# Ten steps' probabilities turned by VectorE and HBM instead of TensorE, with a new order of all instructions

## The chip, the cores and the metric

The kernel runs on one core of one Trainium2 chip. The metric is the device time of one execution in microseconds (us), as the median of several runs; less is better. The core's engines have their own queues and wait for each other only through semaphores: TensorE (PE in the profile, its weight loads PEld), VectorE (DVE), ScalarE (ACT), GpSimd (POOL) and SyncE (SP, which only issues transfers).

## What is computed

Four batches of 768 positions go through attention with 8 heads of 64, and the result through a layer of 512 to 1024 to 512.

```python
k_sum = k.reshape(B, H, nb, 32, D).max(axis=3)
v_sum = v.reshape(B, H, nb, 32, D).mean(axis=3)
# local keys: |i - j| < 16; summary keys: 24 blocks of 32
a = softmax(concat([masked q k^T / 8, q k_sum^T / 8 + log(32)]))
x = a @ concat([v, v_sum])              # 3072 rows of 512
h = x @ w_in                            # 512 -> 1024
solu = h * softmax(h)
out = (layernorm(solu) * g_ln) @ w_out  # 1024 -> 512
```

## The kernel before

**Tiles.** The 3072 rows are 24 tiles of 128. The attention has 24 steps: for each batch `b` and each group `g` of four windows of 64 queries there are two steps `pp`, with two head pairs each; step number 2(3b + g) + pp. A step has `scores` (L649): 16 small products of 64 queries against 96 window keys and 24 block maxima, eight reductions on VectorE that add the mask and take the row maximum (L703), eight exponentials with row sums on ScalarE (L715), a reciprocal, and one multiply that normalises all 128 x 960 probabilities `e` (GpSimd or VectorE). `values_turn` (L753) then turns `e` with 16 transposes on TensorE into a PSUM tile `t` (L751), and two copies bring it to `at` in SBUF. `values` (L774) multiplies `at` with the window's values `vt` (x). `combine` (L831) makes the operands of the wide product from x.

**Wide products.** `first` (L950) and `first_two` (L967, for two tiles at once, from tile 6 on) compute h; hu, hl and hf are its three PSUM banks. `solu` (L1025) does softmax, product and layer norm. From tile 4 on the normalised rows go to HBM and come back turned: `send` (L1084) transposes 32 x 32 blocks on VectorE into a staging tile `tb` and writes it to `far`; `fetch` (L1094) reads it back with four transfers into `lt`, and `rows_split` (L1103) splits it into a rounded part `lh` and a rest `ll`. `second_parts` (L1144) is the output product o, 24 wide products a tile. All wide products take three terms for precision, so both weight matrices are split as well: `rounded` (L458) unpacks a weight tile `raw` into `cv` with a shift (L490) and an integer add (L494), and `split_w_in` and `split_w_out` make the two parts `w` of it.

**Order.** Every operation is recorded by `op` with the engines that may do it and a cost. `Plan.ORDER` is a list of all operations' numbers, written out in the kernel, and `Plan.OTHERS` names those that go to another than their first engine. `Plan.order` (L301) walks the list once with the costs; what it computes only decides where `issue` puts filler products (L1350, products of zeros) on TensorE. Each engine then has its instructions in the list's order, and so has SyncE its transfers: an instruction that waits holds up all behind it on its engine. `buf` gives tiles out of rings of fixed size: two `e`, two `at`, one `tb`, two `vrow` (rows whose block means GpSimd adds up, L599, and space for the weights before). SyncE issues the loads and the far transfers; ScalarE issues the output transfers and six small ones.

Of the kernel before, what the change touches and what calls it, by code (L numbers as in the profile page):

```python
# [10 lines left out]
F32 = mybir.dt.float32  # L11
# [9 lines left out]
P = 128  # L21
# [24 lines left out]
FARK, BACK = 1.6, 2.3  # L46
# [7 lines left out]
WPT = 2  # L54

# [7 lines left out]
class Buf:  # L63


    def __init__(self, make, prev=()):
        self.make, self.prev, self.tile = make, prev, None
        self.ops, self.writers, self.readers, self.gone = [], {}, {}, False
# [8 lines left out]
class Op:  # L77
    def __init__(self, can, deps, prio, nbytes, port, land):
        self.can, self.deps, self.engine, self.fn, self.port = can, deps, None, None, port
        self.first = next(iter(can))  # L80
        self.prio, self.nbytes, self.end, self.start = prio, nbytes, None, None
        self.late, self.land = 0.0, land


class Plan:
# [7 lines left out]
    SMALL = 40.0  # L93
    LANDS = (15.0, 0.5), (50.0, 1.4), (1e9, 1.9)
# [5 lines left out]
    ORDER = [35, 2, 4, 5, 8, 6, 7, 12, 3, 1, 21, 13, 23, 0, 137, 22, 14, 25, 24, 138, 9, 27, 40, 15, 26, 42, 29, 41,  # L100
# [105 lines left out]
        "act": (166, 167, 224, 374, 375, 461, 526, 527, 625, 644, 784, 804, 963, 1082, 1083, 1101, 1102, 1241, 1242, 1538,  # L206
            1557, 1669, 1789, 1790),
    }

    def __init__(self):  # L210
# [1184 lines left out]
```

## Time and profile before

| | before |
|---|---|
| median of 3 runs | 354.65 us (354.13 to 354.76) |
| span of the profiled execution | 353.1 us |
| its whole time | not recorded apart; the median lies 1.55 us above this span |
| busy: PE, DVE, ACT, POOL | 344.2, 292.6, 267.9, 195.2 us |
| transfers | 70.29 MB, mean 199 GB/s |

The span runs from the first instruction to the last. Busy time of TensorE counts each product's whole duration, and products overlap, so the chain of waits tells better how long a block of products takes: in the chain, a piece has its start, its length, and the engine and line that the end of the kernel depended on. Rows of a group of instructions give the line, the engine, the tile written and read, the shape, the count, the busy time, and the mean of one in ns. Names keep the program's tile names, with the buffer numbers left out.

### The profile page before, as it was taken

What the parts mean: (1) busy time and instruction counts of PE and PEld (TensorE: products, weight loads), DVE (VectorE), ACT (ScalarE), POOL (GpSimd) and SP (SyncE); (2) the same over time, 40 slices, a digit from 0 to 9 for tenths busy, and PEclk for the clock granted to TensorE, in tenths of its full rate; (3) what the DMA queues carried; (4) which work ended last, traced back from release to release, by engine and by line L of the source; (5) the groups of instructions that cost most, each with busy time, mean ns of one, the idle gap of its engine ahead of it and who ended that gap; (6) DMA issues with size and microseconds to landing.
All of it is one profiled execution on the core that took longest, in us unless ns stands there. A gap on an engine that the chain in (4) does not pass through costs nothing.

```text
span 353.1 us, 9309 instructions
## 1 busy us (share of the span) xinstructions
PE 344.2 (97%) x3253; PEld 271.0 (77%) x3260; DVE 292.6 (83%) x979; ACT 267.9 (76%) x784; POOL 195.2 (55%) x331
## 2 busy tenths in 40 slices
PE   7799999999999999999999999999999999999995
PEld 3347577778777788888888888887887878888885
DVE  3989999999999798889897998987968988966331
ACT  3799999999988988997877785895884886455410
POOL 5133567797895587849598378237336355031500
PEclk9999999999999999999999999999999999999999
DMA  7999995430259577457559742762834543364611
GB/s 270 375 416 403 324 405 188 148 101 22 97 184 317 190 232 230 163 179 234 156 183 292 253 131 106 252 218 81 270 116 156 198 143 121 114 212 154 207 59 61
DMA packets 29970, 70.29 MB, mean 199 GB/s; under 512 B 4012, under 2 KB 14508, under 8 KB 28388
## 3 DMA queue, kind: packets, MB, share of 16 engines
q1 hardware_dynamic: 26060, 62.96, 53.2%
q10 hardware_dynamic: 3864, 6.74, 5.4%
q8 instruction: 26, 0.43, 0.5%
q14 instruction: 20, 0.16, 0.1%
HBM read 50.60 MB, written 16.78 MB: 191 GB/s over the span
## 4 chain that ended last, share of the span: by engine, by line
PE 88%; DVE 5%; DMA 3%; SPq 1%; issue 1%; POOL 0%; DVEq 0%
PE o L1157 35%; PE hu L980 14%; PE h L961 8%; PE hl L980 7%; PE x L808 6%; PE s L682 6%; PE t L751 4%; PE hf L980 3%; DMA st_v<-in_vr 3%; PE x L1350 1%; PE vs_ps L569 1%; DVE e L703 1%; DVE he L1052 1%; DVE ws_own L383 1%; DVE cv L383 1%
## 5 line engine op out<-in xcount | busy, mean ns | idle before, releaser
L1157 PE MATMUL o<-w,lh 128*128 128x512 f32 (+1 forms) x400 | 131.0, 386 | 0.0
L1157 PEld LDWEIGHTS o<-w,lh 128*128 128x128 f32 x400 | 74.1, 188 | 15.7 <-DVE he L1052 0.2
L1157 PE MATMUL o<-w,ll 128*128 128x512 f32 (+1 forms) x200 | 76.3, 381 | 0.0
L715 ACT ACTIVATE e<-e,nm 128x120 f32<-128x120 f32 x192 | 73.3, 388 | 1.9 <-DVE nm L703 1.7
L1157 PEld LDWEIGHTS o<-w,ll 128*128 128x128 f32 x200 | 37.6, 188 | 6.6
L703 DVE CUSTOM_DVE_ANT_0 e<-s,mask 128x120 f32<-128x120 f32 x192 | 40.7, 276 | 1.5 <-PE s L682 1.3
L384 POOL TENSOR_TENSOR e<-e,z 128x960 f32<-128x960 f32 x15 | 28.1, 1873 | 19.5 <-DVE z L728 18.6
L715 ACT ACTIVATION_READ_ACCUMULATOR e<-e,nm 128x1 f32 x192 | 37.0, 193 | 0.0
L961 PE MATMUL h<-w,xh 128*128 128x512 f32 x96 | 33.6, 405 | 0.0
L384 POOL TENSOR_TENSOR ll<-lt,lh 128x512 fp32r<-128x512 f32 x18 | 23.7, 1322 | 15.9 <-ACT lh L376 14.2
L376 ACT CAST lh<-lt 128x512 fp32r<-128x512 f32 x39 | 23.0, 612 | 8.5 <-PE o L1157 4.0
L1044 ACT ACTIVATE he<-hs,hm 128x512 f32<-128x512 f32 x27 | 19.4, 721 | 12.5 <-DVE hm L1033 12.4
L376 ACT COPY at<-t 120x512 f32<-120x512 f32 x40 | 21.8, 590 | 8.2 <-PE t L751 8.0
L1087 DVE STREAM_TRANSPOSE tbl<-he 128x1024 f32<-128x1024 f32 x20 | 24.7, 1233 | 3.2 <-ACT he L1064 1.7
L808 PEld LDWEIGHTS x<-at,vt 120*64 120x64 f32 (+1 forms) x768 | 24.2, 138 | 3.9 <-issue 3.2
L808 PE MATMUL x<-at,vt 120*64 120x64 f32 (+1 forms) x768 | 26.1, 224 | 0.0
L1067 ACT ACTIVATE sq<-he 128x1024 bf16<-128x1024 f32 x24 | 25.3, 1055 | 0.4
L1165 ACT ACTIVATE os<-o,y 128x512 f32<-128x512 f32 x21 | 14.3, 682 | 14.5 <-PE o L1157 8.9
L384 POOL TENSOR_TENSOR xl<-sums,xh 128x256 fp32r<-128x256 f32 (+1 forms) x14 | 12.6, 899 | 21.3 <-DVE xh L377 18.5
L383 DVE TENSOR_TENSOR ll<-lt,lh 128x512 fp32r<-128x512 f32 x22 | 16.8, 779 | 9.0 <-ACT lh L376 8.9
L1071 POOL TENSOR_SCALAR ss<-ss 128x1 f32<-128x1 f32 x24 | 6.2, 259 | 30.3 <-ACT sq L1067 28.9
L611 POOL TENSOR_TENSOR st_v<-st_v 96x512 f32<-96x512 f32 (+3 forms) x28 | 22.4, 803 | 0.5
(184 smaller groups left out, 863.2 us busy)
## 6 DMA issues: line engine op xcount, KB each, us to landing
vt<-in_v SPq DMA_DIRECT2D x12, 1024.0 KB
farl<-tbl SPq DMA_DIRECT2D x20, 512.0 KB
lt<-farl SPq DMA_DIRECT2D x80, 128.0 KB
kraw<-in_k SPq DMA_DIRECT2D x16, 400.0 KB
out<-os ACTq DMA_DIRECT2D x23, 256.0 KB
qt<-in_q SPq DMA_DIRECT2D x11, 512.0 KB
raw<-in_w_in SPq DMA_DIRECT2D x8, 512.0 KB
raw<-in_w_out SPq DMA_DIRECT2D x8, 512.0 KB
```

The lines of the kernel that those rows point to most:

```text
L376: by = {act: lambda: nc.scalar.copy(out=to(), in_=of()), dve: lambda: nc.vector.tensor_copy(out=to(), in_=of()), pool: lambda: nc.gpsimd.t ...
L383: by = {dve: lambda: nc.vector.tensor_tensor(out=to(), in0=a(), in1=b(), op=kind), pool: lambda: nc.gpsimd.tensor_tensor(out=to(), in0=a() ...
L384: pool: lambda: nc.gpsimd.tensor_tensor(out=to(), in0=a(), in1=b(), op=kind)}
L611: op(pool, 0.15 + w * 0.0021, lambda w=w, o=o: nc.gpsimd.tensor_tensor(out=o.ap[:n, :w], in0=x.ap[:n, :w], in1=x.ap[:n, w:2 * w], op=ALU.add),
L703: nc.vector.tensor_tensor_reduce(out=e.ap[:, n, :], in0=scs[i * each].ap[:, j, (2 * i + up) * KC:(2 * i + up + 1) * KC], in1=mask[:, mi, : ...
L715: nc.scalar.activation(out=e.ap[:, n, :], in_=e.ap[:, n, :], func=AF.Exp, bias=nm.ap[:, n:n + 1], scale=-1.0, accum_out=z.ap[:, n:n + 1])
L808: nc.tensor.matmul(xp()[j * D:(j + 1) * D, i, qs], vs.ap[:k, u, cs], at.ap[:k, u % 2, n[j] + u // 2, :], start=not apart, stop=not apart o ...
L961: nc.tensor.matmul(hp.ap, a.ap[:, c, ts], w.ap[:, i], start=(c == 0 and n == 0), stop=(c == NKC - 1 and n == 2))
L980: nc.tensor.matmul(to.ap, operand(y, n)[:, c], w(c).ap(i), start=first and c == 0 and k == 0, stop=c == 1 and k == 2, skip_group_check=True)
L1067: op(act, 1.05, lambda: nc.scalar.activation(out=sq.ap, in_=e.ap, func=AF.Square, accum_out=ss.ap), r=[e], w=[sq, ss])
L1087: op(dve, 1.17, lambda: nc.vector.transpose(out=tb.ap.rearrange("p (q c a) -> p q c a", q=4, a=32), in_=of().rearrange("p (c q a) -> p q c ...
L1157: nc.tensor.matmul(o.ap[:, cols], a.ap[:, f, :], w.ap[:, i, cols], start=(f == 0 and n == 0), stop=(f == NFC - 1 and n == 2))
```

## The change

Steps from `TURN_FAR` = 14 on no longer call `values_turn`. A new function sends their probabilities the way that the layer's rows already go: one VectorE transpose of 32 x 32 blocks into a staging tile, one transfer to HBM, and four transfers back into one of two fixed tiles `at_far`, which are zeroed once where a half of the queries sees no key of a strip. The four strips of 32 rows are three strips of window keys and the 24 summary keys. `values` then reads 64 queries as two pieces of 32 columns. The two slots of `e` become fixed tiles (`kept`) with 8 columns of zeros behind them.

```diff
+    def far_turn(b, g, pp):
+        e = es.pop((b, g, pp))
+        nm_ = f"{b}_{g}_{pp}"
+        if not turned:
+            for i, slot in enumerate(plan.take_out("at", 2)):
+                y = plan.put(sb, [P, 4, 256], F32, slot, f"at_far{i}")
...
+        y = turned[(2 * (NG * b + g) + pp) % 2]
+        def strips():
+            x = e.ap
+            return bass.AP(x.tensor, x.offset, [x.ap[0], [32, 4], [KC, 8], [1, 32]])
+        d = send(e, strips, f"e{nm_}")
+        rows = d_rows(d)
+        for q, halves, k in ((0, slice(0, 4, 2), 32), (1, slice(0, 4), 32), (2, slice(1, 4, 2), 32), (3, slice(0, 4), KC - WIN)):
+            op(sp, 0.46, lambda q=q, halves=halves, k=k: nc.sync.dma_start(
+                out=y.ap[32 * q:32 * q + k, halves], in_=rows(q)[:k, halves]), r=[d], w=[(y, q)],
+               nbytes=k * len(range(4)[halves]) * 1300)
...
+        def of(u, n, k):
+            if far_:
+                return at.ap[:k, 2 * (u % 2):2 * (u % 2) + 2, 32 * n:32 * n + 32]
+            return at.ap[:k, u % 2, n, :]
...
-            steps = [i for i in (t + 2, t + 3) if i < NT and i != PAIRED + 2]
+            steps = [i for i in (t + 2, t + 3) if i < NT and i != PAIRED + 2 and i < TURN_FAR]
...
+            for i in (t + 4, t + 5):
+                if TURN_FAR <= i < NT:
+                    far_turn(*step(i))
```

From tile 6 on the staging tile is one of two, which alternate; the second is one of the two `vrow` slots:

```diff
+    own["tb"] = plan.take_out("tb") + plan.take_out("vrow")
...
+        if "tb" in own:
+            own["tb"] = own["tb"][::-1]
+            tb = plan.put(sb, [P, DF], F32, own["tb"][0], f"tb{name}")
```

SyncE issues the output transfers of all tiles but the last, and all of the small transfers of `mean_values_pe` and `load_v2`. `mean_values` moves a batch's means with two transfers instead of eight, into a tile of HBM. The shift and the add of a weight tile are one instruction:

```diff
-        op(dve, 0.34, lambda: nc.vector.tensor_scalar(
-            out=high(), in0=high(), scalar1=3, scalar2=None, op0=ALU.logical_shift_left),
-            w=[(st, 0)], port=True)
-        tt(ADD_W, ALU.add, high, high, low, r=[(st, 1)], w=[(st, 0)], port=True)
+        op(dve, 0.66, lambda: nc.vector.scalar_tensor_tensor(
+            out=high(), in0=high(), scalar=3, in1=low(), op0=ALU.logical_shift_left, op1=ALU.bitwise_or),
+            r=[(st, 1)], w=[(st, 0)], port=True)
...
-            op(act, 0.42, lambda os=os, cols=cols: nc.scalar.dma_start(
-                out=out[t * P:(t + 1) * P, cols], in_=os.ap[:, cols]), r=[key], nbytes=int(P * 2048 * k), land=1.2 - 6.55 * k)
+            e, queue = (act, nc.scalar) if t == NT - 1 else (sp, nc.sync)
```

The costs in `Plan` are other ones, and `ORDER` and `OTHERS` are new throughout, so every engine's order differs. Counted over the orders, instructions of some kinds:

| kind | before: DVE, ACT, POOL | now: DVE, ACT, POOL |
|---|---|---|
| conversions of raw weights | 16, 26, 6 | 11, 20, 17 |
| casts to lh | 9, 39, 0 | 7, 23, 17 |
| copies from t to at | 8, 40, 0 | 3, 25, 0 |
| transposes into a staging tile | 20, 0, 0 | 30, 0, 0 |
| transfers issued | 0, 31, 0 | 0, 2, 0 |

On TensorE before, the turns of steps 16 and 17 (t2_2_0 and t2_2_1) stand inside the wide product of tiles 14 and 15 (hu14):

```order
L980 MATMUL hu14_3247<-ws3_141,xl2_1_3206 128x512
L980 MATMUL hu14_3247<-ws3_141,xh2_1_3203 128x512
L751 MATMUL t2_2_0_3365<-ident_68,e2_2_0_3129 120x64 x16
L751 MATMUL t2_2_1_3384<-ident_68,e2_2_1_3274 120x64 x16
L980 MATMUL hu14_3247<-w1s_1825,xh2_1_3203 128x512
L980 MATMUL hu14_3247<-w1s_1825,xl2_1_3206 128x512
```

In the changed kernel no such rows stand there; the same steps appear on TensorE only with their values (x2_2), behind the scores of the next pair (s3_0), and read the staging tiles that transfers fill:

```order
L1217 MATMUL o10_3342<-w15_1099,ll10_3184 128x512
L1217 MATMUL o10_3342<-w15_1099,lh10_3172 128x512
L704 MATMUL s3_0_0_0_3424<-kw3_0_0_3286,qt3_0_2721 64x120 x16
L704 MATMUL s3_0_1_0_3444<-kw3_0_1_3329,qt3_0_2721 64x120 x16
L862 MATMUL x2_2_0_3475<-at_far0_2784,vt2_2_3186 64x64 x16
L862 MATMUL x2_2_1_3499<-at_far1_2798,vt2_2_3186 64x64 x16
```

So two small blocks fewer lie between wide products there, and the values wait for SyncE's transfers in place of the copies.

On VectorE in the changed kernel the two turns of steps 16 and 17 (tbe) stand among the additions of tile 14 (hs14) and behind the operands made from x2_1:

```order
L386 CAST xh22_1_3261<-sums2_1_3168 128x512
L1145 STREAM_TRANSPOSE tbe2_2_0_3271<-kepte_0_2641 128x1024
L750 RECIPROCAL z2_2_1_3221<-z2_2_1_3221 128x8
L1044 ISA hs14_3280,hx14_0_3297<-hf14_3275,hs14_3280 128x512
L1044 ISA hx14_0_3297 128x1
L1145 STREAM_TRANSPOSE tbe2_2_1_3310<-kepte_1_2625 128x1024
```

An addition of tile 14 now stands behind the first of the two transposes, which itself waits for the multiply of `kept`.

On SyncE the program's first loads before are keys, queries, then value rows and weights in turn:

```order
L540 DMA kraw0_1_154<-in_k 128x800 x2
L557 DMA st_v0_0_104<-in_vr 128x1024
L455 DMA raw2_99<-in_w_in 128x1024
L455 DMA raw1_98<-in_w_in 128x1024
L557 DMA st_v0_1_105<-in_vr 128x1024
L455 DMA raw0_97<-in_w_in 128x1024
L557 DMA st_v0_2_106<-in_vr 128x1024
```

and now, from the seventh on:

```order
L547 DMA kraw0_1_156<-in_k 128x800
L464 DMA raw0_97<-in_w_in 128x1024
L464 DMA raw8_124<-in_w_out 128x1024
L564 DMA st_v0_0_104<-in_vr 128x1024
L464 DMA raw2_99<-in_w_in 128x1024
L464 DMA raw7_109<-in_w_in 128x1024
L641 DMA qt0_1_110<-in_q 128x1024
L564 DMA st_v0_1_105<-in_vr 128x1024
L564 DMA st_v0_2_106<-in_vr 128x1024
```

Two more weight tiles (raw3 first of all, and raw1) stand ahead of this piece; the three tiles of value rows (st_v) moved behind weights, and a query tile behind which nothing waits at once stands ahead of two of them.

## Rows read from the trace of the kernel before

**Rows 1.** The page's head, busy totals, and GB/s in 40 slices of 8.83 us.

```profile
span 353.1 us, 9309 instructions
...
PE 344.2 (97%) x3253; PEld 271.0 (77%) x3260; DVE 292.6 (83%) x979; ACT 267.9 (76%) x784; POOL 195.2 (55%) x331
...
GB/s 270 375 416 403 324 405 188 148 101 22 97 184 317 190 232 230 163 179 234 156 183 292 253 131 106 252 218 81 270 116 156 198 143 121 114 212 154 207 59 61
```

**Rows 2.** Stretches: length, busy PE, PEld, DVE, ACT, POOL, clock, DMA share, GB/s.

```profile
28.37:56.30 27.93, 27.88 (x277) 19.68 (x283) 27.29 (x104) 27.36 (x86) 14.22 (x16) 1.00 0.93 340
56.30:72.00 15.70, 15.48 (x150) 11.46 (x154) 15.61 (x46) 14.86 (x39) 12.50 (x14) 1.00 0.51 188
...
190.00:300.00 110.00, 110.00 (x1112) 90.77 (x1112) 95.67 (x332) 83.39 (x256) 57.50 (x107) 1.00 0.53 177
```

**Rows 3.** The chain in order of time (start, length), blocks of TensorE.

```profile
49.23 0.98 PE s L682 x32
50.21 1.08 PE x L808 x32
...
195.83 1.80 PE s L682 x64
197.63 2.02 PE x L808 x64
...
215.52 1.08 PE t L751 x32
216.60 1.59 PE hu L980 x6
218.19 1.36 PE hl L980 x6
...
221.59 1.80 PE s L682 x64
...
316.91 32.29 PE o L1157 x165
```

**Rows 4.** The same chain in the start and the weights stage.

```profile
5.41 11.04 DMA st_v<-in_vr
...
19.76 1.83 PE vs_ps L569 x4
...
28.37 3.62 PE h L961 x15
...
38.27 0.66 PE x L1350 x3
```

**Rows 5.** Groups of instructions, different shapes apart: busy us, mean ns, idle before.

```profile
L715 ACT ACTIVATE e<-e,nm 128x120 f32<-128x120 f32 x192 | 73.3, 388 | 1.9 <-DVE nm L703 1.7
...
L715 ACT ACTIVATION_READ_ACCUMULATOR e<-e,nm 128x1 f32 x192 | 37.0, 193 | 0.0
...
L384 POOL TENSOR_TENSOR e<-e,z 128x960 f32<-128x960 f32 x15 | 28.1, 1873 | 19.5 <-DVE z L728 18.6 <-ACT w L507 0.8
...
L1087 DVE STREAM_TRANSPOSE tbl<-he 128x1024 f32<-128x1024 f32 x20 | 24.7, 1233 | 3.2 <-ACT he L1064 1.7 <-DMA farl<-tbl 1.2 <-issue 0.2
...
L376 ACT COPY at<-t 120x512 f32<-120x512 f32 x40 | 21.8, 590 | 8.2 <-PE t L751 8.0
...
L1052 DVE SCALAR_TENSOR_TENSOR he<-hs,hz,he 128x512 f32<-128x512 f32 x27 | 20.0, 757 | 0.1
...
L383 DVE CUSTOM_DVE_ANT_0 cv<-cv 128x1024 uint16<-128x1024 uint16 x12 | 7.9, 685 | 0.7 <-ACT cv L482 0.5
...
L490 DVE TENSOR_SCALAR cv<-cv 128x512 int32<-128x512 int32 x16 | 6.7, 418 | 0.8 <-ACT cv L467 0.8
```

**Rows 6.** SyncE's queue at the last tile: its write, then its four reads.

```profile
328.24 0.34 SPq L1091 DMA_DIRECT2D farl<-tbl  x1
330.94 1.73 SPq L1097 DMA_DIRECT2D lt<-farl  x4
```

More of the change, by code (lines that the diff above doesn't have):

```diff
@@ L45 @@
 FARS = 8
-FARK, BACK = 1.6, 2.3
 FAR_TO = 24
@@ L54 @@
 WPT = 2
+TURN_FAR = 14
 LATE_ROWS = 0.3
@@ L81, in __init__ @@
         self.prio, self.nbytes, self.end, self.start = prio, nbytes, None, None
-        self.late, self.land = 0.0, land
+        self.late, self.land, self.beside = 0.0, land, []
 class Plan:
     RATES = (6.9, 270.0), (30.0, 410.0), (60.0, 405.0), (1e9, 410.0)
-    SMALL = 40.0
-    LANDS = (15.0, 0.5), (50.0, 1.4), (1e9, 1.9)
+    LANDS, REACH = ((30.0, 0.95, 0.0), (1e9, 1.4, 1e-6)), 0.5
     START = 0.7
@@ L225, in buf @@
         ring.append(b)
+        b.bank = tag == "s"
         return b
@@ L278, in op @@
         assert not any(b.gone for b, _ in r + w)
+        for b in {b for b, _ in r if b.bank and engine != "pe"}:
+            for p in b.ops:
+                if p.first != "pe":
+                    p.beside.append(o)
+                    o.beside.append(p)
         for b, part in r:
@@ L301, in order @@
     def order(self):
-        free, begun, landed, dma, held, lock, kind, done = {}, {}, [0.0] * 8, 0.0, 0.0, 0.0, None, set()
+        free, begun, landed, dma, held, lock, kind, done = {}, {}, [0.0] * 8, 0.0, (0.0, 0.0), (0.0, 0.0), None, set()
         engine = {i: e for e, those in self.OTHERS.items() for i in those}
@@ L312, in order @@
             last = free.get(e, self.START)
-            t = o.start = max([landed[-8] if e == "sp" else 0.0, begun.get(e, self.START) if e == "act" and o.nbytes else last] + [
-                d.end + (0.0 if d.engine == e == "pe" else self.SYNC) for d in o.deps])
+            t = o.start = max([landed[-8] if o.nbytes else 0.0, begun.get(e, self.START) if e == "act" and o.nbytes else last] + [
+                d.end + (0.0 if d.engine == e == "pe" else self.SYNC) for d in o.deps] + [
+                d.end + self.SYNC for d in o.beside if d in done and d.engine != e])
             begun[e] = t
             turn = self.TURN if e == "pe" and kind not in (None, o.kind) else 0.0
-            other = lock if e == "dve" and o.port else held if e == "pool" else 0.0
-            o.end = t + (o.cost + turn) * (2 if e == "pe" and t < self.COLD else 1) + max(other - t, 0.0)
+            o.end = t + (o.cost + turn) * (2 if e == "pe" and t < self.COLD else 1)
+            rival, (a, z) = ("pool", lock) if e == "dve" and o.port else ("dve", held) if e == "pool" else (None, (0.0, 0.0))
+            if a <= t < z:
+                o.end += z - t
+            elif t < a < o.end and o.port:
+                free[rival] = free.get(rival, self.START) + o.end - a
             if e == "pe":
@@ L324, in order @@
             if e == "dve" and o.port:
-                held = o.end
+                held = t, o.end
             if e == "pool" and o.port:
-                lock = o.end
+                lock = t, o.end
             if o.nbytes:
-                dma = max(dma, o.end + 1.0)
-                own = o.end + 1.0 + o.nbytes / self.SMALL * 1e-3
+                dma = max(dma, o.end + self.REACH)
                 dma += o.nbytes / next(r for t, r in self.RATES if dma <= t) * 1e-3
-                o.end = (own if e == "act" else dma) + (o.land or next(x for t, x in self.LANDS if dma <= t))
-                if e == "sp":
-                    landed.append(o.end)
+                o.end = dma + (o.land or next(a + b * o.nbytes for t, a, b in self.LANDS if dma < t))
+                landed.append(o.end)
         return order
@@ L594, in mean_values_pe @@
         for g in range(4):
-            op(act, 0.75, lambda g=g: nc.scalar.dma_start(
+            op(sp, 0.6, lambda g=g: nc.sync.dma_start(
                 out=y.ap[WIN + 6 * g:WIN + 6 * g + 6, :], in_=rows.ap[32 * g:32 * g + 6, :]),
-               r=[rows], w=[(y, g)], nbytes=6 * 2048)
+               r=[rows], w=[(y, g)], nbytes=6 * 2290)
     def add_rows(b, hh, i):
@@ L620, in mean_values @@
     def mean_values(b):
-        vsum[b] = y = plan.buf(sb, [P, DM], F32, "vsum", 1, f"vsum{b}")
-        for h in range(H):
-            x, p0 = vacc[b, h // 4], h % 4 * NB
-            op(sp, 0.76, lambda h=h, x=x, p0=p0: nc.sync.dma_start(
-                out=y.ap[WIN:KC, h * D:(h + 1) * D], in_=x.ap[p0:p0 + NB, :]), r=[x], w=[(y, h)], nbytes=NB * 256)
+        vsum[b] = y = plan.buf(far, [NB, DM], F32, "means", 2, f"vsum{b}")
+        for hh in range(2):
+            x = vacc[b, hh]
+            op(sp, 0.8, lambda hh=hh, x=x: nc.sync.dma_start(
+                out=y.ap.rearrange("n (x h d) -> x h n d", x=2, d=D)[hh], in_=x.ap[:4 * NB, :]),
+               r=[x], w=[(y, hh)], nbytes=4 * NB * 556, land=1.9)
     def load_q(b, g, pairs=None, after=()):
@@ L632, in load_q @@
         part = slice(None) if pairs is None else slice(2 * pairs, 2 * pairs + 2)
-        op(sp, 0.43, lambda: nc.sync.dma_start(out=x.ap[:, part], in_=q[b, g, :, part]),
+        op(sp, 0.46, lambda: nc.sync.dma_start(out=x.ap[:, part], in_=q[b, g, :, part]),
            w=[x] if pairs is None else [(x, 2 * pairs), (x, 2 * pairs + 1)],
-           nbytes=P * 4096 if pairs is None else P * 2048, after=after)
+           nbytes=P * 4270 if pairs is None else P * 2290, after=after)
     def load_v(b, g, after=()):
         vt[b, g] = x = plan.buf(sb, [P, G, DM], F32, "vt", 2, f"vt{b}_{g}")
-        op(sp, 0.43, lambda: nc.sync.dma_start(out=x.ap, in_=v[b, g]), w=[x], nbytes=P * 8192,
+        op(sp, 0.46, lambda: nc.sync.dma_start(out=x.ap, in_=v[b, g]), w=[x], nbytes=P * 8192,
            after=after)
@@ L643, in load_v2, with blocks_of @@
         x, y = vt[b, g], vsum[b]
-        e, cost, queue = (sp, 0.86, nc.sync) if b else (act, 0.8, nc.scalar)
-        return op(e, cost, lambda: queue.dma_start(
-            out=x.ap[WIN:KC], in_=y.ap[WIN:KC, :].rearrange("p (o c) -> p o c", o=1).broadcast_to([NB, G, DM])),
-            r=[y], w=[(x, 1)], nbytes=NB * 8192 * 4, land=None if b else 5.3 - 3 * NB * 8192e-3 / plan.SMALL)
+        return op(sp, 0.88, lambda: nc.sync.dma_start(
+            out=x.ap[WIN:KC], in_=(y.ap[WIN:KC, :] if b < 2 else y.ap[:, :]).rearrange(
+                "p (o c) -> p o c", o=1).broadcast_to([NB, G, DM])),
+            r=[y], w=[(x, 1)], nbytes=NB * 12000)
+    kept = []
+    def blocks_of(e):
+        return e.ap[:, :8 * KC].rearrange("p (n k) -> p n k", k=KC)
     def scores(b, g, pp, direct=False, each=False):
@@ L667, in scores @@
         scs = [plan.buf(ps, [P, 2, 512], F32, "s", 2, f"s{nm_}_{i}") for i in range(1 + each)]
-        e = plan.buf(sb, [P, 8, KC], F32, "e", 2, "e" + nm_)
+        number = 2 * (NG * b + g) + pp
+        if number < TURN_FAR:
+            e = plan.buf(sb, [P, 8 * KC + 32 - NB], F32, "e", 2, "e" + nm_)
+        else:
+            if not kept:
+                for slot in plan.take_out("e", 2):
+                    own_e = plan.put(sb, [P, 8 * KC + 32 - NB], F32, slot, "kept" + slot)
+                    kept.append(own_e)
+                    op(pool, 0.1, lambda own_e=own_e: nc.gpsimd.memset(own_e.ap[:, 8 * KC:], 0.0), w=[(own_e, 2)])
+            e = kept[number % 2]
         nm = plan.buf(sb, [P, 8], F32, "nm", 2, "nm" + nm_)
@@ L703, in reduce @@
                 nc.vector.tensor_tensor_reduce(
-                    out=e.ap[:, n, :], in0=scs[i * each].ap[:, j, (2 * i + up) * KC:(2 * i + up + 1) * KC],
+                    out=blocks_of(e)[:, n, :], in0=scs[i * each].ap[:, j, (2 * i + up) * KC:(2 * i + up + 1) * KC],
                     in1=mask[:, mi, :], scale=-SCALE, scalar=3.0e38,
@@ L772, in values_turn @@
         ats[b, g, pp] = at
+    def far_turn(b, g, pp):
[4 more added lines that the diff above has]
+                y = plan.put(sb, [P, 4, 256], F32, slot, f"at_far{i}")
+                turned.append(y)
+                for q in (0, 2):
+                    op(pool, 0.45, lambda y=y, q=q: nc.gpsimd.memset(
+                        y.ap[32 * q:32 * q + 32].rearrange("p (c o) n -> p c o n", o=2)[:, :, 1 - q // 2], 0.0), w=[(y, q)])
+        y = turned[(2 * (NG * b + g) + pp) % 2]
[8 more added lines that the diff above has]
+               nbytes=k * len(range(4)[halves]) * 1300)
+        ats[b, g, pp] = y
+        far_steps.add((b, g, pp))
+    turned, far_steps = [], set()
     def values(b, g, pp, t=NT, apart=False):
@@ L1168, in second_parts @@
                    out=os.ap[:, cols], in0=o.ap[:, cols], scalar1=y.ap, scalar2=None, op0=ALU.mult))])
-            op(act, 0.42, lambda os=os, cols=cols: nc.scalar.dma_start(
-                out=out[t * P:(t + 1) * P, cols], in_=os.ap[:, cols]), r=[key], nbytes=int(P * 2048 * k), land=1.2 - 6.55 * k)
+            e, queue = (act, nc.scalar) if t == NT - 1 else (sp, nc.sync)
+            op(e, 0.46, lambda os=os, cols=cols, queue=queue: queue.dma_start(
+                out=out[t * P:(t + 1) * P, cols], in_=os.ap[:, cols]), r=[key], nbytes=P * 2290 * k, land=2.0 if t == NT - 1 else None)
     its = [(b, g) for b in range(B) for g in range(NG)]
@@ L1185, in attn_then_solu @@
         first_loads[x].pop(0)()
-    op(sp, 0.43, lambda: nc.sync.dma_start(out=g_sb, in_=g_ln), w=[g_b], nbytes=P * 64)
+    op(sp, 0.46, lambda: nc.sync.dma_start(out=g_sb, in_=g_ln), w=[g_b], nbytes=P * 64)
     for pp in range(NPP):
@@ L1306, in turns @@
         def turns():
-            steps = [i for i in (t + 2, t + 3) if i < NT and i != PAIRED + 2]
-            chain([run(values_turn(*step(i))) for i in steps])
+            steps = [i for i in (t + 2, t + 3) if i < NT and i != PAIRED + 2 and i < TURN_FAR]
+            if steps:
+                chain([run(values_turn(*step(i))) for i in steps])
         behind = second_parts(t - 4 - (t > LATER))
```

61 lines of the change are left out of this document (32 added, 29 removed), and 205 rows, old and new, of tables (ORDER, OTHERS).

## The prediction

> **What bounds the kernel now.** I read the engine totals and the transfer rates by slice first, then the busy time by stretch, then the chain of waits in order of time, then the groups of instructions, and last SyncE's queue. The totals [rows 1] show TensorE busy for 97% of the 353.1 us span, with VectorE second. The stretches [rows 2] split that: from 190 to 300 us TensorE is busy 110.00 of 110.00 us, while VectorE works 95.67, ScalarE 83.39 and GpSimd 57.50. From 28 to 72 us VectorE (27.29 of 27.93, then 15.61 of 15.70) and ScalarE (27.36, 14.86) are as full as TensorE, while GpSimd works 14.22 and 12.50. The chain [rows 3] says the same: in the late stage it is TensorE alone, block after block, and each block that is taken out there should shorten the span by its length. So there are three stages: a start that waits for transfers (to 28 us), a weights stage in which VectorE and ScalarE share the bound with TensorE (to about 130 us), and a stage that TensorE alone bounds. The profiled span is 353.1 us and the median of the runs 354.65, so 1.55 us lie outside the span, and I keep them.
>
> **Turns off TensorE.** Steps 14 to 23 lose their 16 transposes each, that is five pair blocks. One block is 1.08 us, and the wide products behind it start 0.23 us late: six of them take 1.59 instead of 1.36 [rows 3]. 5 x (1.08 + 0.23) = 6.6 us. Nothing covers them, as TensorE is never idle there. **-6.6.**
>
> **Fewer changes between small and wide products.** By the order of instructions TensorE comes back from small blocks to wide ones 35 times before and 25 times now. Five of the ten are the turns above; the other five each save the 0.23 us and what a lone block costs more than half a pair: 0.98 against 1.80 / 2 for scores, 1.08 against 2.02 / 2 for values [rows 3], so 0.07. 5 x 0.30 = 1.5 us. **-1.5.** (That counts two values blocks that are split in two now.)
>
> **What the far path costs.** Each step adds a 1.23 us transpose on VectorE, one write and four reads on SyncE, and takes away two copies of 0.59 us, mostly ScalarE's [rows 5]. VectorE: ten transposes, 12.3 us, hidden as long as it keeps idle time in the last stage (14.3 us from 190 to 300 [rows 2]); rival 2 is the case where it doesn't. The path's latency lies between a step's scores and its values. For the second step of a pair: two times eight exponentials, 16 x (0.388 + 0.193) = 9.3 us, about 0.4 for the first reduction, a multiply of 1.87, the transpose of 1.23 [rows 5], 2.70 from the write's issue to the first read's issue, 1.73 for four reads' issues [rows 6], and for their landing, which no row shows alone, 3 (no less than 0, and taken a little above the write's 2.70, which holds a landing and a queue): 20.2 us. By the order and the blocks of [rows 3], TensorE has 30.0, 25.2, 30.9, 29.2 and 27.3 us of work between those two places for the five pairs. So I take 0, with rival 3 for the other end. The values products read two pieces of 32 columns instead of one of 64; no row shows such a piece; bounds 0 and a doubling of 1.01 us a step [rows 3], taken as 0, since the piece is still a plain run in each partition (rival 4 is the other end).
>
> **Start.** SyncE's list now puts seven weight tiles and a query tile ahead of the third tile of value rows, where three weight tiles stood. In MB: 7.40 instead of 5.31, and 8.97 instead of 6.88 up to the first window values: 2.09 more. At the 0.38 to 0.42 MB/us of the second to fourth slice [rows 1] that is 5.1 us later at most. The value rows are what the chain waits for (11.04 us on that transfer, then the products that average them at 19.76, the first wide product at 28.37 [rows 4]). One scores block of 0.98 us is now done before it, so TensorE loses between 0 and 4.1 us; I take 3, nearer the upper end, as the chain runs through that transfer. **+3.0.** The fillers at TensorE's head (21 instead of 11) delay only the first scores, which wait for their keys anyway.
>
> **Weights stage.** The 16 shifts (0.418) and 16 integer adds (twelve on VectorE at 0.685, four on GpSimd) become 16 fused instructions; no row shows one; the nearest, a fused instruction with a scalar on the same shape, is 0.757 [rows 5]; bounds 0.685, the plain add, and 1.10, both parts. 16 x 0.418 + 12 x 0.685 - 16 x 0.757 = 2.8 us off VectorE (5.0 to -2.7 at the bounds). Eleven conversions also go to GpSimd, and 27 casts over the whole kernel. Counted over the order, at the mean durations of the groups, VectorE's work up to tile 7's normalising product falls from 114.8 to 106.5 us and ScalarE's up to tile 7's square from 144.0 to 135.3. What TensorE can gain there is its own idle time: between the first wide product and tile 1's first output product the order held 16 fillers, now 6 (three take 0.66 us [rows 4]), so 3.5 us, and about 1.3 of waits between 56 and 109 us: 4.8 at most, 0 at least. I take 3.0. **-3.0.**
>
> **Tail.** After the last wide product of the first stage TensorE has 32.29 us of output products now [rows 3]; then 29.9. The last tile's products come 21.8 us after that point instead of 25.8. In the trace its staged rows were issued by 332.67 [rows 6], 15.8 us after it; with landing, cast and subtraction about 19. Cover 2.9 us, cost 0. The output transfers move from ScalarE's queue to SyncE's behind finished tiles; the last two halves stay where they were: 0.
>
> Sum: -6.6 - 1.5 + 3.0 - 3.0 = -8.1; 353.1 - 8.1 + 1.55 = **346.5 us**.
>
> **Rivals.** (1) *The start's delay is not won back.* The rows land 5.1 us late, and the weights stage gives nothing: 354.65 - 8.1 + 5.1 = 351.7. For it: the chain through the transfer. Against it: the weights arrive earlier, and both full engines have 8 us less to do.
>
> (2) *VectorE takes TensorE's place.* Eight of the transposes fall into 190 to 300 us: 95.67 + 9.9, less at most 5.5 if the copies it had go too, is 100.1 to 105.5 in a stretch that should shrink to 103.4. If it also keeps its 14.3 us of waits, the stretch is 114.4 to 119.8 us, 4.4 to 9.8 longer than now, and with the 1.5 saved elsewhere the time is 357.5 to 363, 360 in the middle. It decides above 8.7 us of waits that stay. The Trainium skill, VectorE: DVE Perf Modes, section Rules for kernel authors, would leave a 128 x 128 transpose to TensorE where PSUM can take the result, which speaks for this rival. Against it: over the order, VectorE's work from tile 12 to tile 23 is 125.5 us now and was 127.3, transposes included, since copies, casts and subtractions went to the others.
>
> (3) *The far path comes too late.* Pairs of scores blocks follow each other in 25.8 us (195.83 to 221.59 [rows 3]), in which ScalarE works 19.5 (83.39 in 110 [rows 2]): 9.3 us of exponentials and 10.2 of other work. If all of that stands in between, the 20.2 us become 30.4, and 25.8 for a pair's first step, whose exponentials are 4.6 us shorter. Against the work available (30.0; 25.2; 30.9; 24.1 for step 20, the first of its pair; 27.3) TensorE waits 0.4, 5.2, 0, 1.7 and 3.1 us, 10.4 in all: 357.0, slower. It decides at 8.1 us of waits, 1.6 a pair. Each wait sits in TensorE's queue, with the wide products of the next tiles behind it. For it: SyncE's queue is in order, and reads stand behind others' writes in it. Against it: the exponentials of a pair stand almost together on ScalarE.
>
> (4) *The turns come off, but the values slow down*, as two pieces of 32 columns cost double: +10.1, 356.6.
>
> **Numbers.** My forecast 0.70, rival 1 0.13 (both faster), rival 2 0.04, rival 3 0.07, rival 4 0.02 (all three slower); 0.04 is left for gains and waits that cancel. The forecast's own range is 341.5 (the start costs nothing, the weights stage gives 4.8) to 350. The range over the cases, with rival 1 and part of rival 3, is 341.5 to 353.0. A run can tell 0.2%, 0.7 us, from no change. Faster 0.83, the same 0.04, slower 0.13.
>
> **What would show it.** Right: from about 190 us the chain is TensorE alone, without transposes, with five fewer blocks; tile 14's first wide product to the end of the output products takes about 6 us less; VectorE's busy share from 190 to 300 stays under 95%; the first wide product comes at 30 to 33 us. Wrong: waits of the values products for reads from the staging tiles (rival 3); VectorE full, with TensorE waiting for its additions (rival 2); a values block of two steps well over 2.02 us (rival 4); the first wide product past 33 us and the first of tile 6 no earlier than now (rival 1).

## The result, and the profile of the changed kernel

The changed kernel takes 350.26 us (349.33 to 353.76, 10 runs) against 354.65 before, a ratio of 0.9884 with a 95% interval of 0.9863 to 0.9905: 4.1 us less by the ratio, 4.4 by the medians. The forecast was 346.5 with 341.5 to 353.0 around it. So sign and range held, and half of the forecast gain is missing: the time lies just outside the forecast's own range (341.5 to 350) and nearer to rival 1 (351.7) than to the forecast. The profiled execution has a span of 349.1 us, 1.7 below its own time (350.84). A few executions ran 1 to 2% longer at a mean granted clock of 0.990 to 0.995 (353.76 here; 358.2 to 359.9 in three of nine of the run with more fillers, whose median is taken without them).

The page's head and busy totals of the changed kernel, to be read against [rows 1]:

```profile
span 349.1 us, 9081 instructions
...
PE 340.5 (98%) x3109; PEld 268.6 (77%) x3114; DVE 292.2 (84%) x941; ACT 254.7 (73%) x753; POOL 225.7 (65%) x380
```

TensorE is as full as before, VectorE has the same work, ScalarE has 13 us less and GpSimd 30 more. The stretches (length, busy PE, PEld, DVE, ACT, POOL, clock, DMA share, GB/s):

```profile
32.89:56.30 23.41, 23.41 (x229) 17.09 (x230) 21.31 (x59) 20.83 (x58) 11.56 (x21) 1.00 0.92 336
56.30:72.00 15.70, 15.70 (x164) 12.55 (x162) 14.67 (x47) 14.76 (x40) 12.51 (x16) 1.00 0.41 126
190.00:300.00 110.00, 109.00 (x928) 89.62 (x928) 94.95 (x317) 77.02 (x239) 67.51 (x115) 1.00 0.78 248
```

From 190 to 300 us TensorE now waits for 1.00 us where it waited for nothing [rows 2], and VectorE's busy time has hardly moved, 94.95 instead of 95.67: it took the transposes and gave up other work. The chain of waits in order of time (start, length), to be read against [rows 3, 4]:

```profile
19.48 2.26 PE x L1416 x10
22.13 0.98 PE s L704 x32
23.11 3.54 PE vs_ps L576 x8
...
32.89 4.12 PE h L1015 x18
...
87.20 0.76 DVE he L1106 x2
87.96 1.97 DVE ws_own L392
90.36 0.68 DVE he L1106 x2
91.08 5.06 PE h L1015 x21
...
204.73 5.41 DMA lt<-farl
...
221.47 1.80 PE s L704 x64
223.28 2.02 PE x L862 x64
...
315.56 30.26 PE o L1217 x156
```

Three things stand there. The first wide product (h) comes at 32.89 instead of 28.37 us, behind the averaging of the value rows (vs_ps) and ten fillers (L1416, products of zeros); by the records of its instructions, as in all such times below, it starts at 32.54 instead of 28.30. At 87 to 91 us the chain leaves TensorE for VectorE. And around 205 us it leaves TensorE again, for a transfer of the layer's rows; this third one is of this execution, since in the second profile the chain stays on TensorE from 180 to 260 us. TensorE's waits by what ended them (us in total, times, longest):

```profile
PE hu L1034 <- DVE hx L1044: 1.3, 2, 1.0
PE vs_ps L1416 <- DVE zero L410: 1.3, 1, 1.3
PE h L1015 <- DVE he L1106: 1.1, 1, 1.1
PE hu L1034 <- DVE he L1106: 0.6, 1, 0.6
```

To see where the time went I added up TensorE's instructions in the trace, from the start of one to the start of the next, by what they do. The table is a sum over the trace's records and not a view of the profile. The columns are the kernel before, the changed one, its second profile (first experiment) and the kernel of the second experiment:

```
us of TensorE's time            before   changed   again   turns back
wide products (1122)            258.17   256.19   255.83   257.38
scores, values, value means      58.25    57.84    57.55    57.57
turns (t and lt)                 16.27    11.41    11.33    16.85
fillers                          11.46    15.08    16.24    15.54
waits                             3.78     4.04     2.23     4.83
ahead of the first, past the last 5.13     4.57     4.55     4.35
span                            353.06   349.13   347.73   356.52

fillers and waits, by stage     before   changed   again
to the first wide product        11.42    14.96    15.35
from it to 72 us                  3.55     1.15     1.18
72 to 109 us                      0.27     1.70     1.65
109 to 190 us                     0.00     0.31     0.29
190 us to the end                 0.00     1.00     0.00
```

The work on TensorE fell by 7.3 us (the first three lines), the piece behind its last product by 0.6, and fillers and waits grew by 3.9.

### The profile page after: what moved, and what is told of

It reads as the page before. It is cut to its first block, busy times and chain, and to the rows that moved or that the text cites. A ratio compares the mean times of both kernels' runs of the same rounds, so it can differ in the third digit from the quotient of the medians.

```text
span 349.1 us, 9081 instructions
## 1 busy us (share of the span) xinstructions
PE 340.5 (98%) x3109; PEld 268.6 (77%) x3114; DVE 292.2 (84%) x941; ACT 254.7 (73%) x753; POOL 225.7 (65%) x380
## 4 chain that ended last, share of the span: by engine, by line
PE 83%; DVE 9%; DMA 3%; issue 1%; ACT 1%; POOL 1%; SPq 0%; POOLq 0%
PE o L1217 32%; PE hu L1034 13%; PE h L1015 10%; PE hl L1034 6%; PE x L862 6%; PE s L704 5%; PE hf L1034 3%; PE t L773 2%; DMA lt<-farl 2%; PE vs_ps L576 2%; DMA kraw<-in_k 1%; DVE he L1106 1%; DVE ksum L556 1%; PE x L1416 1%; DVE e L725 1%
## 5 line engine op out<-in xcount | busy, mean ns | idle before, releaser
L737 ACT ACTIVATE e<-e,nm 128x120 f32<-128x120 f32 x112 | 42.7, 389 | 0.0
L1225 ACT ACTIVATE os<-o,y 128x512 f32<-128x512 f32 (+1 forms) x24 | 16.0, 671 | 27.6 <-PE o L1217 24.4
L737 ACT ACTIVATE kepte<-kepte,nm 128x120 f32<-128x120 f32 x80 | 30.5, 386 | 0.0
L725 DVE CUSTOM_DVE_ANT_0 e<-s,mask 128x120 f32<-128x120 f32 x112 | 23.9, 278 | 2.3 <-PE s L704 2.2
L1118 ACT ACTIVATE he<-he,nmu 128x512 f32<-128x512 f32 x29 | 20.3, 719 | 7.7 <-DVE nmu L1109 7.7
L1015 PEld LDWEIGHTS h<-w,xh 128*128 128x128 f32 x96 | 18.0, 188 | 6.6 <-DVE he L1106 1.3
L704 PE MATMUL s<-kw,qt 64*64 64x120 f32 x704 | 21.5, 267 | 0.0
L704 PEld LDWEIGHTS s<-kw,qt 64*64 64x64 f32 x704 | 18.1, 133 | 4.4 <-issue 1.8
L1106 DVE SCALAR_TENSOR_TENSOR he<-hs,hz,he 128x512 f32<-128x512 f32 x27 | 21.0, 800 | 0.3
L1015 PE MATMUL h<-w,xl 128*128 128x512 f32 x48 | 18.7, 390 | 0.0
```

The source lines that it names most:

```text
L704: nc.tensor.matmul(scs[i * each].ap[cu * QT:(cu + 1) * QT, j, c:c + ks.shape[-1]], qs.ap[ds, 2 * pp + i, u * QT:(u + 1) * QT], ks, start=T ...
L725: nc.vector.tensor_tensor_reduce(out=blocks_of(e)[:, n, :], in0=scs[i * each].ap[:, j, (2 * i + up) * KC:(2 * i + up + 1) * KC], in1=mask[ ...
L737: nc.scalar.activation(out=blocks_of(e)[:, n, :], in_=blocks_of(e)[:, n, :], func=AF.Exp, bias=nm.ap[:, n:n + 1], scale=-1.0, accum_out=z. ...
L1015: nc.tensor.matmul(hp.ap, a.ap[:, c, ts], w.ap[:, i], start=(c == 0 and n == 0), stop=(c == NKC - 1 and n == 2))
L1106: op(dve, 0.69 if maxes else 0.67, lambda i=i, hp=hp: nc.vector.scalar_tensor_tensor(out=part(i), in0=hp(), scalar=zs.ap[:, 0:1], in1=part ...
```

## The experiments

**The changed kernel again.** No edit.

> The changed kernel once more, beside the runs below. 350.3 us, a ratio of 0.988 to the kernel before. The wait of 1.0 us on TensorE at 216 us and that of 1.14 at 90 us are in the same place if the order of instructions makes them, and gone or elsewhere if they were that one execution's.

349.62 us (349.34 to 353.64), ratio 0.9882 (0.9849 to 0.9915). TensorE's waits in this profile:

```profile
PE h L1015 <- DVE he L1106: 1.1, 1, 1.1
PE hu L1034 <- DVE he L1106: 0.5, 1, 0.5
PE hu L1034 <- DVE hx L1044: 0.3, 1, 0.3
```

The waits at 90, 108 and 142 us are in the same places and belong to the order. The 1.0 us at 216 is gone, and the span is 1.4 shorter: that wait comes in some executions only.

**Turns back on TensorE.** `values_turn` and its copies return for steps 14 to 23, each pair about six wide blocks ahead of the next scores; the far transfers for `e` go.

```diff
-TURN_FAR = 14
+TURN_FAR = 24
```

> The changed kernel with steps 14 to 23 turned on TensorE again, two copies each on ScalarE, no far transfers for them; the rest of the order is the changed kernel's. Theory A (the turns gave their whole length, and the missing 4 us were lost elsewhere): five pair blocks of 1.08 and five returns of 0.23 come back, +6.6 us, or +5.6 if the late wait of 1.0 us goes with the far path: 355.9 to 356.9. Theory B (VectorE and the far transfers took back what TensorE gave up): +3 or less, 353.3 or below.

356.57 us (356.37 to 358.23), 6.95 above the first experiment and 6.3 above the first median of the changed kernel: theory A. In the table the turns come back with 5.52 us and the wide products with 1.55, 7.07 together. Theory B falls. The late wait does not belong to the far path, since it appears here too, at 218.8 us:

```profile
PE hu L1040 <- DVE hx L1050: 2.0, 2, 1.7
```

The Trainium skill, VectorE: DVE Perf Modes, section Rules for kernel authors, would leave a 128 x 128 transpose to TensorE where PSUM can take the result. Here TensorE is the full engine, and the way past it, by 32 x 32 blocks on VectorE and through HBM, was worth 6.95 us.

**Fewer fillers at the start.** Numbers 42 to 48 of the fillers are left out, ahead of the fourth turn.

```diff
+        fills.append(0)
+        if 41 < len(fills) <= 48:
+            return
```

> The changed kernel with seven of the ten filler products ahead of the fourth turn at 19.5 us left out (1.6 us). What is behind them can start 0.8 us earlier, until it waits for the second tile of value rows. Theory A (a later start goes through to the end): -0.8 us, 349.5. Rival C (the weights stage is held by VectorE and ScalarE, which don't get their work earlier): 0, 350.3.

348.67 us (348.49 to 348.80), 0.95 less than the first experiment: theory A. The first wide product comes 0.9 us earlier, and the same 0.9 is there at tile 6 (105.57 instead of 106.50 us). The fillers' number comes from the planner's estimates, and here seven of them, 1.6 us, covered no more than some 0.7 us of waiting (1.6 - 0.95).

**More fillers at the start.**

```diff
+        for _ in range(17 if len(fills) == 48 else 1):
             nc.tensor.matmul(x[:, :n], zero[:, :P], zero[:, :n], start=True, stop=True)
```

> The changed kernel with 16 more filler products at the same place, 3.6 us by the mean of one there. Theory A: the first wide product moves from 32.9 to 36.5 us and the end by the same 3.6, 353.9. Rival C: the stage up to 109 us has slack on TensorE, and less than 1.5 of it reaches the end, 351.8 or below.

352.9 us, 3.3 above the first experiment: theory A. The first wide product comes 3.4 us later (35.98 instead of 32.59). The wait at 90 us is still 1.13 us long and now stands at 93.4: VectorE, which seemed to hold TensorE there, has moved with it; its instructions there work on TensorE's products (h) and so wait in turn.

**The same delay in the kernel before.** 16 fillers more ahead of its first values block.

> The kernel before with 16 more filler products ahead of its first values block (3.6 us), so that its first wide product comes at 31.9 instead of 28.3 us. If a later start goes through in that kernel too, 358.2 us. If its full VectorE and ScalarE between 28 and 72 us gave TensorE slack there, less than 2 of the 3.6 arrive, 356.6 or below, and the changed kernel's late start would have been cheap in the old order.

357.83 us, 3.3 more than before (ratio 1.0094, 1.0081 to 1.0107), for a first wide product that comes 3.4 us later. A late start was not cheap in the old order either: it passes it on as well.

**Shift and add apart again**, both on VectorE.

```diff
-        op(dve, 0.66, lambda: nc.vector.scalar_tensor_tensor(
-            out=high(), in0=high(), scalar=3, in1=low(), op0=ALU.logical_shift_left, op1=ALU.bitwise_or),
-            r=[(st, 1)], w=[(st, 0)], port=True)
+        def shift_add():
+            nc.vector.tensor_scalar(
+                out=high(), in0=high(), scalar1=3, scalar2=None, op0=ALU.logical_shift_left)
+            nc.vector.tensor_tensor(out=high(), in0=high(), in1=low(), op=ALU.add)
+        op(dve, 0.66, shift_add, r=[(st, 1)], w=[(st, 0)], port=True)
```

> The changed kernel with the fused instruction of a weight tile made two again, the shift (0.418) and the add (0.685), both on VectorE, in place of 0.730 measured: 16 x 0.373 = 6.0 us more on VectorE between 7 and 60 us. If VectorE's load in the weights stage is what sets TensorE's pace there, +3 to +6, 353 to 356. If the start sets it and VectorE has room, under +1, 350.6 or below.

355.17 us (ratio 1.0022, 1.0013 to 1.0030), 4.9 to 5.5 above the two medians of the changed kernel. More than the reckoned 6.0 us came onto VectorE, since both parts took longer here than in the kernel before (in the rows of instructions, the busy time and the mean ns of one stand behind the first bar):

```profile
PE 340.9 (96%) x3109; PEld 268.3 (76%) x3114; DVE 300.3 (85%) x957; ACT 255.2 (72%) x753; POOL 226.4 (64%) x380
...
L502 DVE CUSTOM_DVE_ANT_0 cv<-cv 128x1024 uint16<-128x1024 uint16 x16 | 13.9, 866 | 1.5 <-DVE cv L500 0.2
L500 DVE TENSOR_SCALAR cv<-cv 128x512 int32<-128x512 int32 x16 | 7.4, 461 | 0.0
```

VectorE's busy time is 8 to 9 us above the two profiles of the changed kernel (292.2 and 291.1), so some 60% of what was added arrives. The first wide product is 2.6 us later (35.23 against 32.59), tile 6's 5.5 later (112.02 against 106.50). So a delay of TensorE goes through almost whole, and one of VectorE for the larger part.

**One weight tile later.** raw8 is loaded behind the first window values, its six conversions are moved with it in the list.

> The changed kernel with one weight tile of the output layer (raw8, 0.5 MB, first needed at 64 us) loaded behind the first window values instead of ahead of the value rows, and its six conversions moved behind the first ones of the other tiles. The rows land 1.28 us earlier, VectorE and ScalarE have 3.6 us less to do before 26 us, and the first wide product comes 1.3 to 2 us earlier. Theory A (the start goes through to the end): 347.6 to 348.4. Rival C (the six conversions are then missing room between 27 and 40 us, and the weights stage takes the gain back): 349.6 or above.

350.80 us (ratio 0.9895, 0.9880 to 0.9910): rival C. The first wide product comes 1.9 us earlier, at 30.64, but tile 6's at 106.65, where it was 106.50. What the time is longer by comes later: in this profile TensorE waits 1.1 us at 199 us for far reads. The earlier start that was bought by moving VectorE's and ScalarE's work behind it bought nothing by tile 6; the one that moved nothing (the trimmed fillers) went through.

**The fused instruction alone, in the kernel before**, where VectorE did both parts (12 tiles).

> The kernel before with the shift and the add of a weight tile fused where VectorE did both (12 of 16; the four whose add is GpSimd's stay): 12 x 0.373 = 4.5 us off VectorE, nothing else of the change. If VectorE's load in the weights stage sets the pace, at the 5.2 us for 6.0 that the unfused run showed, -3.9: 350.7. If in the old order TensorE and ScalarE hold that stage as well, 0 to -1.5: 353.1 or above.

354.43 us, ratio 0.9983 (0.9970 to 0.9997): 0.6 us for 3.9 us of VectorE's time (288.7 against 292.6 us busy). In the old order VectorE was not alone, ScalarE was as full there [rows 2]; that this is the reason fits, but no run shows it.

**Every far transpose twice.**

```diff
+                for _ in range(2 if name[0] == "e" else 1):
                     nc.vector.transpose(
```

> The changed kernel with every transpose of the ten far steps' probabilities done twice into the same tile: 10 x 1.24 = 12.4 us more on VectorE after 170 us. If VectorE has the room that its busy share of 86% from 190 to 300 us says (15 us), under +2, 351.6 or below. If its idle time is waiting that stays (rival 2 of the prediction, had the path been a little dearer), +5 to +10, 355 to 360.

356.54 us (ratio 1.0061, 1.0047 to 1.0075), 6.3 to 6.9 more: inside the second expectation. VectorE's idle time of 15 us took less than half of 12.4. TensorE's longest waits in it:

```profile
PE hu L1034 <- DVE hx L1044: 3.9, 5, 1.9
```

The stretches around the longest of them (1.85 us at 217.7), columns as above:

```profile
213.00:219.00 6.00, 4.71 (x21) 3.57 (x19) 6.00 (x9) 0.07 (x1) 5.28 (x7) 1.00 0.67 224
219.00:225.00 6.00, 5.44 (x17) 4.32 (x18) 5.69 (x15) 3.63 (x10) 1.33 (x7) 0.72 0.36 105
```

VectorE is busy 6.00 of 6.00 us while TensorE waits, and then the granted clock falls to 0.72 in the mean: a little over half of the next 6 us ran at 1.2 GHz. That fall is of the profiled execution (357.66 us, clock 0.995 in the mean); the other five kept 1.00 and took 355.8 to 357.0 us, so the clock does not make the 6.3 to 6.9 us.

**Output transfers on ScalarE again.**

```diff
-            e, queue = (act, nc.scalar) if t == NT - 1 else (sp, nc.sync)
+            e, queue = act, nc.scalar
```

> The changed kernel with the output transfers issued by ScalarE again, as before, in the same place of the list. The prediction put this at 0: 349.3 to 350.6. If ScalarE's waits for SyncE's or the transfers' turn hold up its exponentials, +1 or more; if SyncE's list is what makes the far reads late, -1.

360.35 us (ratio 1.0145, 1.0123 to 1.0168), 10 to 11 more than the changed kernel. The sign is that of "+1 or more", but neither its size nor its reason, ScalarE's exponentials. TensorE's two new waits:

```profile
PE x L862 <- DMA at_far<-fare: 4.4, 1, 4.4
PE x L862 <- POOL lh L387: 2.4, 1, 2.4
```

The second row names GpSimd's cast, on which a values block does not depend; what it waits for are the last far reads, issued at 197.9 and 198.7 us. SyncE's waits between 180 and 232 us:

```profile
SPq L814 <- DMA out<-os: 7.1, 1, 7.1
...
SPq L1158 <- DMA out<-os: 4.6, 1, 4.6
```

The stretches with TensorE's two waits:

```profile
197.00:205.00 8.00, 5.56 (x93) 4.63 (x84) 6.94 (x41) 6.80 (x29) 6.27 (x11) 0.82 0.74 231
225.00:240.00 15.00, 10.60 (x135) 9.02 (x128) 11.05 (x52) 7.17 (x30) 4.90 (x10) 0.77 0.63 221
```

ScalarE issues an output transfer later than SyncE would (195.54 instead of 194.82 us for one, 226.69 instead of 222.81 for another), and a read on SyncE waits until that output has landed, 4.6 and 7.1 us. In the trace all transfers tell of their end on eight semaphores in turn, and a transfer waits for the one that had its semaphore before. So it can be held by an earlier one of another queue that it has nothing to do with: the read issued at 229.27 us has the semaphore of the output issued at 226.69, whose last count comes at 229.25. The far reads behind it come too late and TensorE waits 2.44 us at 198.6 and 4.40 at 227.3; its clock falls 1 us after the first wait and within the second, to 0.82 and 0.77 in the mean of the two stretches, where it was 1.00 in the second profile of the changed kernel. This is the prediction's rival 3 in its effect, called forth by an edit; the cause, a semaphore shared with another queue, it had not named. It does not price the move of the outputs by itself, since the list puts the far reads where they suit SyncE's issues.

**Two edits more.** The trimmed fillers, and tile 4's second product on VectorE (number 442 of the list) put directly behind its first (443), ahead of a sum of weights (327) and a copy (534).

> The changed kernel with two small edits: the seven filler products left out (-0.95 in their own run), and tile 4's second product on VectorE put directly behind its first instead of behind a sum of weights that takes 2.05 us and a copy, for which TensorE waits 1.13 us at 90 us in every run. If TensorE's wait is the place where VectorE's order costs time, -1.0 more: 347.6 to 347.9. If VectorE's whole load holds the stage (the sum of weights is then late instead), no more than trimming alone: 348.7.

347.47 us (ratio 0.9793, 0.9767 to 0.9820): faster than both kernels, and 1.2 below trimming alone by the medians. The wait at 90 us is gone, and so is that at 108:

```profile
PE s L711 <- DMA qt<-in_q: 1.6, 3, 0.9
PE vs_ps L1428 <- DVE zero L417: 1.3, 1, 1.3
PE s L711 <- ACT kw L392: 0.5, 1, 0.5
PE hu L1041 <- DVE hx L1051: 0.3, 1, 0.3
```

So the wait came from the place of the sum in the order. On VectorE in the first experiment's profile, and GpSimd beside it:

```profile
87.25 0.75 DVE L1106 SCALAR_TENSOR_TENSOR he<-h,hz,he 128x512 f32<-128x512 f32 x1
87.92 2.05 DVE L392 TENSOR_TENSOR ws_own<-w,w 128x512 f32<-128x512 f32 x1
89.89 0.50 DVE L386 COPY kw<-ksum 128x192 f32<-128x192 f32 x1
90.32 0.74 DVE L1106 SCALAR_TENSOR_TENSOR he<-h,hz,he 128x512 f32<-128x512 f32 x1
...
88.13 1.29 POOL L393 TENSOR_TENSOR ws<-ws_own,ws 128x512 fp32r<-128x512 f32 x1
```

The sum took 2.05 us beside GpSimd's, and 0.69 with GpSimd idle (at 64.27 us in the same profile). The 1.36 us between the two are more than the wait of 1.13, so keeping GpSimd's sum apart might have ended the wait too; no run tried that.

**A third one**: tile 5's second product (508) behind its first (507) too.

> The same, and tile 5's second product put behind its first as well, ahead of two instructions that make the first operands of tile 6 (TensorE waits 0.52 us there, at 108 us). If order alone makes that wait, -0.4 more than the run before it; if the operands are then late, 0 or +0.5.

347.64 us (ratio 0.9790, 0.9766 to 0.9814): no difference. The wait that it was meant for had gone with the edit before.

## Why the prediction held, and which steps were off

**Bound.** Right. From 217 us on the chain is TensorE alone and holds no transposes, and VectorE's busy share from 190 to 300 us is 86%. The stretch from 190 to 217 us, where the chain of the first profile runs through VectorE and a transfer, was not foreseen; it leads to that profile's late wait, and in the second profile TensorE is alone there too.

**Turns off TensorE, -6.6.** Right: 6.3 to 6.95 by the run that puts them back. From tile 14's first wide product to TensorE's last product I named some 6 us less; it is 144.0 before, 141.4 now and 140.1 in the second profile: four pairs' turns lie in it, not five (4 x 1.08 = 4.3), three output products more (0.7 us) lie in it too, and 1.0 of the first profile's is the late wait.

**Fewer changes, -1.5.** Mis-sized together with the turns. By class TensorE's work fell by 7.3 us where the two terms say 8.1. The returns are as counted: leaving fillers out, the trace has 35 before and 25 now, at 0.20 each (258.17 - 256.19 = 1.98). The turns that are left cost 0.5 us more than before (11.41 against 16.27 - 5 x 1.08), the first two of them in four pieces of eight transposes.

**Far path, 0.** Right in the result, wrong in the size of the latency. I reckoned 20.2 us from scores to landed strips for a pair's second step. In the first experiment's profile the last read's issue alone ends 18.0 to 25.2 us after the scores, with 3.2 to 8.2 left to the values block, in which the strips must land. The longest is step 15, whose write was issued at 186.75 in the changed kernel's profile (the one at 182.69 is step 14's):

```profile
182.69 0.34 SPq L1149 DMA_DIRECT2D fare<-tbe  x1
185.49 1.24 DVE L1145 STREAM_TRANSPOSE tbe<-kepte 128x1024 f32<-128x1024 f32 x1
...
186.75 0.32 SPq L1149 DMA_DIRECT2D fare<-tbe  x1
187.16 2.05 SPq L814 DMA_DIRECT2D at_far<-fare  x4
...
191.15 0.90 SPq L814 DMA_DIRECT2D at_far<-fare  x2
192.57 0.79 SPq L814 DMA_DIRECT2D at_far<-fare  x2
```

Its reads stand behind the other step's and a row's reads in SyncE's queue, which is what rival 3 said, and in the run with the later weight tile TensorE did wait 1.1 us for them. It was near: an output transfer on another queue was enough to bring it about.

**Start, +3.0.** Right in kind, a little too small: 3.5 us more of fillers and waits, and the first wide product 4.2 us later by the trace and 4.5 by the chain, inside the 30 to 33 us that I named. By the trace's completion events the third tile of value rows landed at 23.3 instead of 18.9 us, 4.5 later where I said 5.1 at most (six weight tiles stand ahead of it and not seven; the 2.09 MB are right). About 0.9 of the delay were fillers that covered no wait.

**Weights stage, -3.0: this step failed.** It counted less work on VectorE and ScalarE and concluded that "What TensorE can gain there is its own idle time", 3.5 us of fillers and 1.3 of waits. Less than that was there to be gained: six of the 16 fillers stay, so 10 x 0.22 = 2.2 us could go, and the waits from 56 to 109 us were 0.5 us, 0.22 up to 72 us [rows 2] and 0.25 behind it (the kernel before):

```profile
72.00:108.80 36.80, 36.55 (x412) 28.60 (x410) 35.03 (x127) 33.44 (x98) 33.29 (x46) 1.00 0.35 106
```

So 2.7 us were the most, below the 3.0 taken. Fillers and waits from the first wide product to 72 us did fall from 3.55 to 1.15, but those from 72 to 109 us rose from 0.27 to 1.70: -1.0 in all. A sum of work over a stage cannot see this, since the wait at 90 us came from one sum of weights put between two products. Moving it gave 1.2 us back. (The fused instructions were no part of the miss: at the 0.730 us measured they take 3.2 us off VectorE where 2.8 was reckoned; the bound of 5.0 should have been 3.9.) So most of the start's delay arrived at the end, as rival 1 had it, and the delay runs show that neither order absorbs one. The sign that I had named for rival 1, tile 6's first product no earlier than now, doesn't decide: its main block (hu) starts at 108.5 instead of 108.8 us, but six wide products fewer stand ahead of it.

**Late waits, not in the sum.** 0.3 us at 142 us in both profiles of the changed kernel and 1.0 more in the first. **Tail, 0**: 0.6 better, 3.89 to 3.32 us behind the last product.

Together, from the first profile (work, start, weights stage, late waits, and the pieces ahead of the first and behind the last product): -7.25 + 3.54 - 0.97 + 1.31 - 0.56 = -3.93, the difference of the spans (349.13 - 353.06). That the time still fell inside the stated range owes something to luck: its upper part was there for rival 1 and not for a stage that gives a third of its term.

**Rival 2** (VectorE becomes the bound) did not come, but VectorE has little room: 12.4 us more on it cost 6.3 to 6.9. **Rival 4** is out: a product on two pieces of 32 columns takes as long as one on 64 (mean ns of one).

```profile
L862 PE MATMUL x<-at,vt 120*64 120x64 f32 x384 | 13.0, 224 | 0.0
...
L862 PE MATMUL x<-at_far,vt 120*64 120x64 f32 x320 | 10.9, 224 | 0.0
```

What stays open: what the outputs' move is worth in an order made for it, and which part of the old order kept the fused instruction from paying there. Taken back one at a time, the turns (6.3 to 6.95) and the fused instructions (4.9 to 5.5) come to far more than the 4.1 to 4.4 us that the whole change gives. The fused ones alone gave the old order 0.6, so such prices hold for one order and cannot be added up.

## What to carry to other kernels

In a chain of engines that wait for each other, a delay at the start can go through to the end even where another engine looks like the bound, because that engine waits in turn; it did so in both orders here. Test it by adding a delay before counting on a later stage to win it back. Before counting on idle time, see how much of it the new order still holds. Work taken off a full engine may pay little (0.6 us of 3.9 in the old order): look for the instruction that stands between a producer and its consumer, not at the sum. And filler products are a cost where they cover more than the wait (0.95 us here).

## What the runs showed of the hardware

- With waits of TensorE of 2.44 and 4.40 us in the output run, the granted clock fell to its lower level (1.2 GHz) for a part of the stretches around them, behind the first and from within the second; after 1.85 us in the run with double transposes too. After waits of 1.1 and 1.7 us in other runs it stayed at 2.4 GHz. So a wait can cost twice. The output run lost 6.8 us by the two waits and, as an estimate, some 4 by the clock: 8 x 0.18 + 15 x 0.23 = 4.9 us, of which about 1 fell while TensorE still waited.
- A SyncE transfer waited up to 7.1 us for the landing of an unrelated transfer of ScalarE's; for 4.6 of them ScalarE had not issued it yet.
- A sum on VectorE took 2.05 us beside a GpSimd sum of 1.29, and 0.69 alone. The Trainium skill, SBUF — State Buffer, section Who interferes with whom, states that a VectorE instruction with two SBUF inputs contends with a GpSimd instruction that reads SBUF, and that the shared pair of ports is an exclusive lock. 0.69 + 1.29 = 1.98 agrees with a wait for the whole other instruction; VectorE's record starts 0.21 us ahead of GpSimd's, though, so the trace does not show how GpSimd came to be first.
- The fused shift and or took 0.730 us in the mean of 16, near the 0.757 that was taken for it.
